# How dense matmuls are shared out over the attention units, and the order of the last output products

## The chip, the cores and the metric

The kernel runs on one NeuronCore of one Trainium2 chip. The metric is the device time of one execution in microseconds (us). TensorE is called PE in the profile, VectorE DVE, ScalarE ACT, GpSimd POOL, and SyncE SP, which issues most of the transfers (DMAs).

## What is computed

The input x (2048 tokens x 1024) is layer-normed, and the sum of three things is returned: x itself, an attention with a memory over the normed x, and a token-mixing MLP over the normed x. The attention, which the change is about, cut to what matters:

```python
# H = 32 heads of Dh = 32, N = 4 segments of L = 512 tokens; q, k, v from x @ wq, wk, wv
for s in range(N):
    logits = einsum('bhqd,bhkd->bhqk', qs, ks) * scale + mask      # causal inside the segment
    a_dot = einsum('bhqk,bhkd->bhqd', softmax(logits), vs)
    a_mem = einsum('bhld,bhde->bhle', phi(qs), M) / (einsum('bhld,bhd->bhl', phi(qs), z) + 1e-6)
    outs.append(g * a_mem + (1 - g) * a_dot)
    M = M + einsum('bhld,bhle->bhde', phi(ks), vs)
    z = z + einsum('bhld->bhd', phi(ks))
out = x + concat(outs) @ wo + mlp                                   # phi(t) = t+1 if t>0 else exp(t)
```

## The kernel before

The MLP and parts of K come first, for about 374 us; their sum with x is left in DRAM as a half-precision partial result (`part_d`). The attention follows, and the change concerns its second part.

**Units.** Attention runs over 32 units u = 0 to 31. Unit u is segment u // 8 and a group of four heads, u % 8. In unit u the kernel computes the *logits* of unit u and the *weighing* (probabilities times values) of unit u - 1. `logits(u, step)` writes PSUM banks 0 to 3: step 0 is key block 0, step 1 is key blocks 1 and 3, and step 2, only in even units, is key block 2 of units u and u + 1 together. After each, one ACT instruction takes exp from the four banks into `pT` (line 1363), and POOL masks the diagonal blocks of `pT` (line 1367). So each logits step has to wait until the exp of the step before has read the banks.

`weigh(u - 1, part)` for parts 0, 1, 2 writes bank 4, 5, 4. After each part DVE copies the bank to `ost` (line 1414). Part 2 therefore waits until the copy of part 0 has been made. In segments 0 to 2 part 2 also updates the memory (`MZ`, lines 1422 and 1424 on DVE).

**Dense jobs.** Between these small products lie jobs of eight dense 128x128x512 matmuls, in banks 6 and 7 by turns (`self.turn`): `v_job` (values, one for each unit up to 27), `q_job` and `k_job` (projections for unit u + 2; from unit 14 on k is loaded from DRAM by `k_load`), and `wo_job`, which is half of an output row block: eight matmuls of `oT` with `wo`, an addition to `fin` on DVE (line 1306), and, for each second half, a transfer of `fin` to the output and a reload of another `fin` with `load_fin`, both issued by SP. There are 24 output jobs for the first three segments. Job n + 2 uses the bank of job n, so it waits for the instruction that empties it: DVE for `k_job` and `wo_job` (and for some early `v_job`), ACT for `q_job` and `v_job`.

**Order.** Everything is written out by hand in program order. `unit_jobs(u)` says which jobs join the queue in unit u. Units 10 to 17 get one output job, put first. From unit 18 on a quota applies: 24 matmuls in even units and 20 in odd ones, filled up with output jobs, put last; what a job has over the quota stays for the next unit (`self.left`). The last unit takes all that is left. `cut` shares the unit's dense matmuls among the places between the small products. In even units the order of places is: before logits 0, before weighing part 0, before part 1, before part 2, before logits 1, before logits 2, before the next unit. Odd units have no logits 2, so there the sixth number is what lies between logits 1 and the end of the unit.

**Side work.** Each unit also leaves a list of VectorE work in `self.side`: scales, products (`prod`, line 1460) and sum (`o_s`, line 1466) of unit u - 1, then `phi_q` and `phi_k` (lines 1227 and 1229), and in some units `xn_scale` (`xs`, line 1133). One item is issued at each stop of a dense job (`STOPS`, or `STOPS_FEW` from unit 14 on, in matmuls of the job), in the places where side work is allowed. DVE runs all of it in the order of issue, with the bank copies and the additions.

**Tail.** After unit 31 the last segment's output is computed in eight products n = 0 to 7 of `product(n, j0, j1)`, each over eight head groups. Seven groups exist early. The last must wait for the weighing of unit 31, its combination on DVE, a transpose on PE (`o_transpose`) and an ACT copy. When a product is complete, DVE adds it to `fin` (line 1617) and the result goes out.

Of the kernel before, what the change touches and what calls it, by code (L numbers as in the profile page):

```python
# [16 lines left out]
N_SEG = 4  # L17
# [13 lines left out]
N_UNIT = N_SEG * N_GRP  # L31
# [355 lines left out]
class _Kernel:  # L387
# [1098 lines left out]
        fw.op("act", lambda e: e.activation(self.oT[s % 3][:, g, :], bb, ACT.Copy),  # L1486
              reads=[self.R_bank[b]], writes=[self.R_oT[s % 3][g]])

    QUOTA_FROM, QUOTA = 18, (24, 20)
    STOPS = ((1, 4, 7), (1, 4))  # L1490
    STOPS_FEW = ((1, 3, 5, 7), (1, 3, 5))
    XN_AT = (0, 1, 2, 3, 6, 7, 8, 9, 14, 15, 16, 17)

    def unit_jobs(self, u):
        jobs = [self.wo_job(*self.wo_jobs.popleft())] if 10 <= u < self.QUOTA_FROM else []
        m = u // 4 + 1
        if m < 2 * N_SEG:
            jobs.append(self.v_job(m, u % 4))
        if u + 2 < N_UNIT:
            jobs.append(self.q_job(u + 2))  # L1500
            if u + 2 < N_UNIT // 2:
                jobs.append(self.k_job(u + 2))
            else:
                self.k_load(u + 2)
        if u >= self.QUOTA_FROM:
            quota = self.QUOTA[u % 2] if u + 1 < N_UNIT else 100
            quota -= 8 * len(jobs) + sum(8 - j[0] for j in self.jobs)
            while quota > 0 and self.wo_jobs:
                jobs.append(self.wo_job(*self.wo_jobs.popleft()))
                quota -= 8  # L1510
            self.left = max(-quota, 0)
        return jobs

    def k_load(self, u):
# [3 lines left out]
    def attention(self):  # L1518
        self.jobs, self.turn, self.left = deque(), 0, 0
        self.side, self.stops = deque(), self.STOPS  # L1520
        self.exps, self.in_etmp = [], [None] * 4
        self.wo_jobs = deque((c, half) for c in range(4 * (N_SEG - 1)) for half in range(2))
        self.jobs.extend([self.q_job(0), self.k_job(0)] + [self.v_job(0, c) for c in range(4)])
        self.dense(16)
        self.late_exps()
        self.phi_k(0)
        self.k_transpose(0)
        self.jobs.extend([self.q_job(1), self.k_job(1)])
        self.dense(100)
        for u in range(N_UNIT):  # L1530
            if u == N_GRP:
                t, R = _Walk(self.mem, self.B_AT + self.STG_AT, self.B_AT + self.S2_AT).take(
                    "oT2", [P, N_GRP, SEG_L], BF16, N_GRP)
                self.oT.append(t)
                self.R_oT.append(R)
                self.load_fin(0)
                self.load_fin(1)
            if 1 <= u <= N_GRP:
                self.fw.dma(self.wo[:, u - 1, :], self.A_wo[(u - 1) * P:u * P, :], writes=[self.R_wo[u - 1]])
            even = u % 2 == 0  # L1540
            self.jobs.extend(self.unit_jobs(u))
            total = 8 * len(self.jobs) - sum(j[0] for j in self.jobs) - self.left
            xn = self.XN_AT.index(u) + 4 if u in self.XN_AT else None
            if u in self.XN_AT[::4]:
                self.xn_load(xn)
                self.xn_load(xn + 1)
            if u < 10 or u >= 14 and total <= 26:
                cuts = self.cut(total, (0, 4, 2, 4, 1, 13, 8) if even else (7, 3, 2, 4, 1, 15))
            else:
                cuts = self.cut(total, (0, 4, 2, 2, 2, 14, 8) if even else (7, 3, 2, 2, 2, 16))  # L1550
            end = u >= N_UNIT - 4
            self.stops = self.STOPS_FEW if total <= 26 and u >= 14 else self.STOPS
            self.dense(cuts[0])
            self.logits(u, 0)
            self.dense(cuts[1], end)
            while end and self.side:
                self.side.popleft()()
            if u:
                self.weigh(u - 1, 0)
            self.dense(cuts[2], False)  # L1560
            if u:
                self.weigh(u - 1, 1)
            self.dense(cuts[3], False)
            if u:
                self.weigh(u - 1, 2)
                steps = self.combine(u - 1)
                last = steps[-1]
                steps[-1] = lambda u=u, last=last: (last(), self.o_transpose_dma(u - 1))
                self.side.append(steps.pop(0))
            if N_GRP <= u:  # L1570
                self.side.append(lambda u=u: self.phi_q(u))
            if u:
                self.side.extend(steps)
            if u + 1 < N_UNIT:
                self.side.append(lambda u=u: (self.phi_k(u + 1), self.k_transpose(u + 1)))
            if xn is not None:
                self.side.append(lambda c=xn: (self.xn_scale(c), self.xn_transpose(c), c % 4 < 2 and self.xn_load(c + 2)))
            self.dense(cuts[4])
            self.logits(u, 1)
            if even:  # L1580
                self.dense(cuts[5])
                self.logits(u, 2)
            self.dense(8 * len(self.jobs) - sum(j[0] for j in self.jobs) - self.left)
        while self.side:
            self.side.popleft()()
        self.tail()
# [10 lines left out]
    def tail(self):  # L1597
        fw = self.fw
        s, u = N_SEG - 1, N_UNIT - 1
        fin, R_fin = self.fin, self.R_fin  # L1600
        for i in range(2, 4):
            self.load_fin(4 * s + i)
        fw.wait_outputs(3)

        def product(n, j0, j1, cols=((0, 512),)):
            i, h, b = n // 2, n % 2, (0, 1, 2, 3, 6, 7, 5, 4)[n]
            for p, (c0, c1) in enumerate(cols):
                with fw.group(reads=self.R_wo[j0:j1] + self.R_oT[s % 3][j0:j1], writes=[self.R_bank[b]]):
                    for jc in range(j0, j1):
                        fw.mm(self.ps[:, b, c0:c1], self.oT[s % 3][:, jc, i * P:(i + 1) * P],  # L1610
                              self.wo[:, jc, h * 512 + c0:h * 512 + c1], start=(jc == 0), stop=(jc == N_GRP - 1))
                if j1 < N_GRP:
                    return
                dst = fin[i][:, h * 512 + c0:h * 512 + c1]
                R = Res("fin")
                R.w = R_fin[i][h].w
                fw.op("dve", lambda e: e.tensor_tensor(dst, self.ps[:, b, c0:c1], dst.bitcast(F16), op=ALU.add),  # L1617
                      reads=[self.R_bank[b], R], writes=[R])
                fw.dma(self.out_d[:, 4 * s + i, h * 512 + c0:h * 512 + c1], dst, reads=[R],
                       is_output=True, issuer=("sp", "act")[p % 2])  # L1620
                b = (b + 1) % 3

        product(0, 0, 6)
        product(1, 0, 6)
        self.weigh(u, 0)
        self.weigh(u, 1)
        product(2, 0, 6)
        self.weigh(u, 2)
        for step in self.combine(u):
            step()  # L1630
        product(3, 0, 6)
        for n in range(3):
            product(n, 6, 7)
        product(4, 0, 7)
        self.o_transpose(u, 4)
        product(3, 6, 7)
        product(5, 0, 7)
        for n in range(6):
            product(n, 7, 8)
        product(6, 0, 8)  # L1640
        product(7, 0, 8, ((0, 256), (256, 384), (384, 512)))

# [27 lines left out]
```

## Time and profile before

| what | value |
|---|---|
| time, median of three runs | 654.52 us (654.16, 654.52 and 1095.52) |
| the profiled execution | 654.28 us |
| its span in the profile | 652.2 us, 11204 instructions |
| matmuls of 128x512, mean as the profile models it | 380 ns |
| exp, line 1363 | 80 times, mean 1877 ns |
| mask on POOL, line 1367 | 128 times, mean 847 ns |
| `prod` on DVE, line 1460 | 24 times, 1215 to 1680 ns |
| addition to `fin` on DVE, line 1306 | 24 times, mean 682 ns |
| granted TensorE clock | 1.0 |

The attention's units begin at 387.48 us in the span, and the tail at about 633.9 us. Matmuls overlap in the pipeline, so the difference of two starts tells more than the durations. In a timeline each row gives the start, the length, the engine, the line, what is written and read, and the number of merged instructions.

### The profile page before, as it was taken

The page shows a single profiled execution, that of the slowest core. Times are in us where ns is not written, and L with a number is a line of the kernel's source. Part 1 is how long each engine was busy: PE and PEld are TensorE (multiplying, and loading weights), DVE is VectorE, ACT ScalarE, POOL GpSimd, SP SyncE. Part 2 cuts the span into 40 slices and gives each one's busy share as a digit, 9 for nine tenths or more (in the row PEclk, how much of TensorE's full clock was granted, in tenths as well). Part 3 has the DMA queues.
Part 4 walks back from the last instruction along what each step waited for, and adds up shares of the span by engine and source line. Part 5 has one row for each costly group of instructions (what it writes and reads, how often), then busy time and mean ns, then how long its engine had stood idle before and what let it go on. Part 6 is the DMA issues. An engine that isn't in the chain of part 4 may idle for free.

```text
span 652.2 us, 11204 instructions
## 1 busy us (share of the span) xinstructions
PE 646.7 (99%) x4611; PEld 303.1 (46%) x4611; DVE 439.9 (67%) x829; ACT 281.5 (43%) x305; POOL 154.9 (24%) x181
## 2 busy tenths in 40 slices
PE   9999999999999999999999999999999999999998
PEld 3444444444444444444444444444545444454444
DVE  6975775665655673745637325767898988887895
ACT  7542232232210000111101047778767788888760
POOL 2500000000011220120201203434333445544450
PEclk9999999999999999999999999999999999999999
DMA  8804242242498937629263956979644576355424
GB/s 300 217 0 130 65 116 79 65 124 70 129 265 216 231 96 210 171 87 258 66 193 116 257 136 156 190 182 227 124 120 109 152 164 144 90 115 123 114 81 138
DMA packets 190123, 95.00 MB, mean 146 GB/s; under 512 B 108664, under 2 KB 176248, under 8 KB 190072
## 3 DMA queue, kind: packets, MB, share of 16 engines
q1 hardware_dynamic: 189928, 94.25, 56.9%
q8 instruction: 36, 0.59, 0.4%
q14 instruction: 15, 0.12, 0.1%
q10 hardware_dynamic: 144, 0.03, 0.0%
HBM read 69.23 MB, written 11.53 MB: 124 GB/s over the span
## 4 chain that ended last, share of the span: by engine, by line
PE 90%; DVE 4%; DMA 2%; ACT 1%; POOL 1%; issue 1%; DVEq 0%
PE ps_all L199 90%; ACT pT L1363 1%; DMA w2s<-in_B_w_dram 1%; POOL pT L1367 1%; DVE fin L1617 1%; DVE ln_st L590 1%; DVE sum L651 0%; DVE prod L1460 0%; DMA xin<-in_A_x_dram 0%; DVE h L630 0%; POOL ln_rs L614 0%; DVE mtmp L1229 0%; DVE mtmp L1227 0%; DVE ost L1414 0%; DVE part L692 0%
## 5 line engine op out<-in xcount | busy, mean ns | idle before, releaser
L1363 ACT ACTIVATE pT<-ps_all 128x2048 bf16<-128x2048 f32 x80 | 150.2, 1877 | 47.2 <-PE ps_all L199 46.8
L1367 POOL TENSOR_SCALAR_AFFINE_SELECT pT<-pT 128x512 bf16<-128x512 bf16 x128 | 106.3, 847 | 160.9 <-ACT pT L1363 160.9
L692 DVE TENSOR_TENSOR part<-ps_all,part 128x512 f32<-128x512 f32 x84 | 57.7, 690 | 108.9 <-PE ps_all L199 88.2
L1078 POOL TENSOR_TENSOR part<-part,stg 128x512 f32<-128x512 f32 x24 | 33.0, 1402 | 285.0 <-DVE part L692 268.1
L749 ACT ACTIVATE g<-part,b1c 128x512 f16<-128x512 f32 x36 | 26.0, 722 | 99.0 <-DVE part L692 99.0
L199 PE MATMUL ps_all<-wv,xnT 128*128 128x512 bf16 x256 | 68.2, 380 | 0.2
L199 PE MATMUL ps_all<-xnT,wq 128*128 128x512 bf16 x256 | 65.6, 380 | 0.0
L199 PE MATMUL ps_all<-wo,oT 128*128 128x512 bf16 (+2 forms) x272 | 64.3, 367 | 0.2 <-ACT pT L1363 0.2
L1414 DVE CAST ost<-ps_all 128x396 bf16<-128x396 f32 (+2 forms) x96 | 44.3, 473 | 27.3 <-PE ps_all L199 26.6
L697 ACT ACTIVATE part<-ps_all 128x512 f32<-128x512 f32 x24 | 14.0, 596 | 101.4 <-PE ps_all L199 67.1
L199 PEld LDWEIGHTS ps_all<-vA,pT 128*128 128x128 bf16 x1280 | 45.5, 96 | 21.5 <-DVE ost L1414 3.3
L199 PE MATMUL ps_all<-g,sum 128*128 128x512 f16 x224 | 51.0, 379 | 0.0
L199 PE MATMUL ps_all<-g,w2s 128*128 128x512 f16 x224 | 51.0, 379 | 0.0
L199 PE MATMUL ps_all<-gT,sum 128*128 128x512 f16 x224 | 50.3, 379 | 0.1
L199 PE MATMUL ps_all<-vA,pT 128*128 128x33 bf16 x1280 | 48.5, 178 | 0.7 <-POOL pT L1367 0.6
L199 PE MATMUL ps_all<-h,sum 128*128 128x512 f16 x192 | 45.2, 379 | 0.0
L199 PE MATMUL ps_all<-h,w1s 128*128 128x512 f16 x192 | 44.9, 379 | 0.0
L199 PE MATMUL ps_all<-hT,sum 128*128 128x512 f16 x192 | 43.6, 379 | 0.0
L199 PEld LDWEIGHTS ps_all<-wo,oT 128*128 128x128 bf16 x272 | 23.8, 97 | 27.1 <-issue 4.9
L1460 DVE TENSOR_TENSOR prod<-ost,srec 128x1024 bf16<-128x1024 bf16 x24 | 35.1, 1461 | 0.0
L199 PEld LDWEIGHTS ps_all<-gT,sum 128*128 128x128 f16 x224 | 21.8, 98 | 26.8 <-DVE gT L666 0.6
L199 PEld LDWEIGHTS ps_all<-g,w2s 128*128 128x128 bf16 x224 | 21.9, 98 | 26.4
(118 smaller groups left out, 862.2 us busy)
## 6 DMA issues: line engine op xcount, KB each, us to landing
w2s<-in_B_w_dram SPq DMA_DIRECT2D x8, 1792.0 KB, 9.5
w1s<-in_B_w_dram SPq DMA_DIRECT2D x12, 1024.0 KB, 5.6
wq<-in_A_wq_dram SPq DMA_DIRECT2D x32, 256.0 KB, 3.4
xs<-in_A_x_dram SPq DMA_DIRECT2D x24, 256.0 KB, 3.4
stg<-in_A_x_dram SPq DMA_DIRECT2D x16, 256.0 KB, 2.8
out_dram<-stg SPq DMA_DIRECT2D x16, 256.0 KB, 3.8
wk<-in_A_wk_dram SPq DMA_DIRECT2D x16, 256.0 KB, 3.4
fin<-out_dram SPq DMA_DIRECT2D x16, 256.0 KB, 3.3
```

Of the source, the lines that this page charges most:

```text
L199: ins = self.nc.tensor.matmul(*args, **kwargs)
L590: fw.op("dve", lambda e: e.bn_stats(st[:, 6 * h:6 * h + 6], src[:, 512 * h:512 * h + 512]), reads=[self.R_xin[c]], writes=[R])
L692: self.fw.op("dve", lambda e: e.tensor_tensor(self.tmp[dst][:], self.bank(b), self.tmp[src][:], op=ALU.add), reads=[self.R_bank[b], self.R ...
L697: self.fw.op("act", lambda e: e.activation(self.tmp[dst][:], self.bank(b), ACT.Copy), reads=[self.R_bank[b]], writes=[self.R_tmp[dst]])
L749: self.fw.op("act", lambda e: e.activation(self.gB[f % 2][half][:, f // 2, :], src, ACT.Gelu_apprx_tanh, bias=self.b1c[:, f:f + 1], scale= ...
L1078: fw.op("pool", lambda e: e.tensor_tensor(self.tmp[t][:], self.tmp[t][:], self.stg[k][:, 512 * half:512 * half + 512], op=ALU.add), reads= ...
L1363: fw.op("act", lambda e: e.activation(dst, src, ACT.Exp, scale=SCALE), reads=self.R_bank[0:4], writes=[R[v % 2][kb] for v, kb, _ in blocks ...
L1367: fw.op("pool", lambda e: e.affine_select(d, d, pattern=[[0, 4], [1, P]], compare_op=ALU.is_ge, fill=0.0, base=0, channel_multiplier=-1), ...
L1414: fw.op("dve", lambda e: e.tensor_copy(dst, src), reads=[self.R_bank[b]], writes=[self.R_ost[o][part]])
L1460: fw.op("dve", lambda e: e.tensor_tensor(self.prod[:], ost[:, :, 0:D_HEAD], rec.unsqueeze(2).to_broadcast([P, 32, D_HEAD]), op=ALU.mult), ...
L1617: fw.op("dve", lambda e: e.tensor_tensor(dst, self.ps[:, b, c0:c1], dst.bitcast(F16), op=ALU.add), reads=[self.R_bank[b], R], writes=[R])
```

## The change

Four things change. Output jobs from unit 10 on all go by quotas, given in rows of four by u % 4: 28 in units 10 to 13, then 24, 24, 24, 20 in units 14 to 21 (20 where u % 4 is 3), then 24 in every unit from 22 to 30. Output jobs are put behind the others, except that in units 28 and 29 the first two jobs change places. From unit 14 on, even units give one matmul more to the place before weighing part 0, and one less to the place before logits 2. In the tail the first product goes to the dense bank that is next in turn instead of bank 0, the others move up accordingly, and product 5 is split after its fifth group, so that the last groups of products 0 to 4 are computed before the rest of it.

```diff
-    QUOTA_FROM, QUOTA = 18, (24, 20)
+    WO_FROM, QUOTA = 10, ((28, 28, 28, 28), (24, 24, 24, 20), (24, 24, 24, 24))
...
     def unit_jobs(self, u):
-        jobs = [self.wo_job(*self.wo_jobs.popleft())] if 10 <= u < self.QUOTA_FROM else []
-        m = u // 4 + 1
+        jobs, m = [], u // 4 + 1
...
-        if u >= self.QUOTA_FROM:
-            quota = self.QUOTA[u % 2] if u + 1 < N_UNIT else 100
+        if u >= self.WO_FROM:
+            quota = self.QUOTA[(u >= 14) + (u >= 22)][u % 4] if u + 1 < N_UNIT else 100
             quota -= 8 * len(jobs) + sum(8 - j[0] for j in self.jobs)
             while quota > 0 and self.wo_jobs:
                 jobs.append(self.wo_job(*self.wo_jobs.popleft()))
                 quota -= 8
             self.left = max(-quota, 0)
+            if m >= 2 * N_SEG and u + 2 < N_UNIT:
+                jobs[0:2] = jobs[1::-1]
...
-            if u < 10 or u >= 14 and total <= 26:
+            if u >= 14 and total <= 26:
+                cuts = self.cut(total, (0, 5, 2, 4, 1, 12, 8) if even else (7, 3, 2, 4, 1, 15))
+            elif u < 10:
                 cuts = self.cut(total, (0, 4, 2, 4, 1, 13, 8) if even else (7, 3, 2, 4, 1, 15))
...
-            i, h, b = n // 2, n % 2, (0, 1, 2, 3, 6, 7, 5, 4)[n]
+            i, h, b = n // 2, n % 2, (6 + self.turn, 0, 1, 2, 3, 7 - self.turn, 5, 4)[n]
...
         product(3, 6, 7)
-        product(5, 0, 7)
-        for n in range(6):
+        product(5, 0, 5)
+        for n in range(5):
             product(n, 7, 8)
+        product(5, 5, 8)
```

## The prediction

> **What bounds the kernel now.** I read the busy shares first, then TensorE's waits, then the chain of waits for the second half, then the timelines of TensorE and VectorE unit by unit.
>
> ```profile
> PE 646.7 (99%) x4611; PEld 303.1 (46%) x4611; DVE 439.9 (67%) x829; ACT 281.5 (43%) x305; POOL 154.9 (24%) x181
> ...
> PE ps_all L199 <- POOL pT L1367: 0.6, 3, 0.3
> PE ps_all L199 <- ACT pT L1363: 0.4, 2, 0.2
> ```
>
> TensorE (PE) is the bound, and the change neither adds nor removes a matmul. Only idle slivers between matmuls can move. The recorded waits are 1.0 us together, but ends of matmuls are modelled, so I measured slivers by starts. Eight dense matmuls back to back take 1.73 us from start to start (0.216 each), a logits block of four to eight takes 0.33, and a step from dense work to logits costs 0.09. What a row takes beyond that is a stall. The chain shows where stalls lie:
>
> ```profile
> 530.92 1.69 DVE prod L1460
> 532.63 0.74 DVE o_s L1466
> 533.37 0.46 DVE xs L1133
> 533.83 0.49 DVE ost L1414
> 534.36 11.84 PE ps_all L199 x133
> ...
> 588.48 1.89 ACT pT L1363
> 590.43 1.35 POOL pT L1367
> 591.92 11.21 PE ps_all L199 x148
> ...
> 631.86 1.89 ACT pT L1363
> 633.89 8.91 PE ps_all L199 x78
> 643.02 2.60 PE ps_all L199 x12
> 646.21 3.60 DVE fin L1617 x7
> ```
>
> Four kinds are to be seen. (1) At 534.36 the last weighing of unit 18 waits for VectorE (DVE) to empty the bank of the first weighing, because VectorE is still on the combination of the unit before. Such waits: 0.18 (unit 15), 0.20 (16), 0.21 (18), 0.09 each (20, 24), together 0.77; and 0.21 in unit 11 for the bank that the kT copy empties. (2) At 588.48 exp runs after an odd unit's second logits; the next logits need its end, and the weighing then needs the mask of POOL. (3) At 631.86 the first tail product needs bank 0, which the last exp still reads. (4) At 646.21 the final additions run back to back on VectorE to the end.
>
> Kind 2 has a measurable rule: from the second logits to the next logits at least 0.45 to the start of exp, 1.88 of exp, 0.14 to the next logits, 2.47 us in all. Nine dense matmuls between give 0.33 + 1.94 + 0.09 = 2.36, so 0.10 is lost; ten give 2.58 and nothing is lost:
>
> ```profile
> 602.70 0.40 PE L199 MATMUL ps_all<-qT,kT 32*128 32x384 bf16 x8
> ...
> 605.17 0.40 PE L199 MATMUL ps_all<-qT,kT 32*128 32x512 bf16 x4
> ...
> 609.00 0.40 PE L199 MATMUL ps_all<-qT,kT 32*128 32x384 bf16 x8
> ...
> 611.60 0.40 PE L199 MATMUL ps_all<-qT,kT 32*128 32x256 bf16 x8
> ```
>
> 605.17 minus 602.70 is 2.47 (nine between), 611.60 minus 609.00 is 2.60 (ten).
>
> **The Trainium skill.** "TensorE: Matmul & The Clock Gate", Back-to-back issue gap, gives N/2.4 + 2.5 ns for a matmul, 216 ns at 512 columns; the trace agrees (0.216). "PSUM — Partial Sum Buffer", Engine vs sequencer instructions: the queues of ScalarE, VectorE and GpSimd are strict FIFO. The chain above agrees: the bank's copy stood 2.9 us behind prod, o_s and xs (530.92 to 533.83). "SBUF — State Buffer", Who interferes with whom: a VectorE instruction with two SBUF inputs and a GpSimd instruction that reads SBUF block each other whole. The trace agrees: prod takes 1.22 us where it starts before the mask and 1.65 to 1.68 where the mask came first.
>
> **The change, part by part.** Worked through by hand, the quotas give the dense matmuls per unit: units 10 to 13, 32 before and 28 after; 15, 24 and 20; 21, 23, 25, 27 and 29, 20 and 24; the others and unit 31 (16) unchanged. That is -16 -4 +20 = 0: 0.216 x 0 = 0.
>
> Longer odd units. Units 21 to 29 get 11 instead of 9 between logits. Five stalls of 0.10 go: -0.50. The later weighing of units 26, 28 and 30 now comes at 0.33 + 2.38 + 0.09 + 0.33 + 0.86 = 3.99 after the logits, and the mask is ready at 591.92 - 588.03 = 3.89. So the mask waits go too, with 0.10 to spare: 0.44, 0.43 and 0.43 (each with the small wait ahead of it), and 0.16 in unit 22, where the dense bank came late from ScalarE: -1.46. Late next is VectorE, below.
>
> One more ahead of the weighing. In even units of 24 the cuts go from 0, 3, 1, 4, 0, 10, 6 to 0, 4, 1, 3, 1, 9, 6. The three ahead of the last weighing still sum to 8, so VectorE's waits there don't feel it, but the ten between second and third logits become nine: by the rule above 0.10 in each of units 14, 16, ... 30, nine times: +0.90. Unit 15, now of 20, pays the same: +0.10.
>
> VectorE in units 11 to 24. The output products come last in a unit instead of first, so their addition (0.60 start to start) lands at other places in VectorE's queue, and 4 fewer or 2 fewer matmuls cover the same queue. Each wait is counted from weighing to weighing. Unit 18: product O5 ends just before its first weighing, so its addition stands ahead of the bank's copy besides xs: 0.21 + 0.60 = 0.81. Unit 16: an addition for xs (+0.14), two matmuls fewer (+0.43), 0.10 of it already paid: 0.67. Unit 15: the same addition, two matmuls fewer: 0.18 + 0.33 = 0.51. Units 12 and 14: two matmuls fewer against a margin of 0.12 and 0.09: 0.31 and 0.34. Units 22 and 24: a new addition (+0.60), two matmuls more (+0.43, of which the stalls just removed take 0.26 and 0.10): 0.60 - 0.17 - 0.12 of slack = 0.31, and 0.09 + 0.60 - 0.33 = 0.36. Unit 20 keeps 0.09. Sum 3.40 for 0.77: +2.63. In unit 11 the kT copy has only the queue of one K job ahead and eight matmuls of cover; I take its 0.21 as gone: -0.21. From unit 26 on, the last weighing has no state update, VectorE idled before the copy, and the added 0.60 costs nothing; if that idle time were gone it would cost up to 0.6 each.
>
> Tail. The first product goes to the bank of the last-but-one output job, whose addition ended at 631.80, long before 633.6: the stall of 0.33 (2.15 for eight matmuls, less 1.73 and 0.09) goes. Its own six matmuls cover exp's end for the second product. The split lets the first final addition start two matmuls (0.43) earlier; the ScalarE copy of the last oT ends at 643.66, and the six matmuls left as cover end at 642.86 + 1.30 = 644.16, so no wait. But the last addition can't start before the last matmul ends at 649.53, against 649.73 now: only 0.17 of the 0.43 counts. -0.50.
>
> Moved with each output job: an output transfer and a reload of fin on SP for each second one. Up to unit 27 they come later than before, from unit 28 at the same place; no PE wait in this stage ends on them, and the first products of the second segment move from unit 18 to 21, away from the oT they need. The swap in units 28 and 29 only exchanges q and an output job. Nothing for either; without that cover a reload (SP issue to landing, 3.3 us) would hold VectorE.
>
> **Sum.** -0.50 - 1.46 + 0.90 + 0.10 + 2.63 - 0.21 - 0.50 = +0.96. The profiled run took 654.28 with a span of 652.2, so 2.1 lie around it, and it stands 0.24 below the median of 654.52. 654.28 + 0.96 = 655.2.
>
> Bounds of what the trace doesn't show: the VectorE waits could stay as they are (-2.63 from the sum, 652.6), since the order of additions may shift by one copy; that they vanish (-0.77 more) I exclude, as no addition leaves the queue of units 15 to 18 without matmuls leaving too, or they could rise by prod taking 1.67 where it takes 1.22 (0.45 in each of units 12 and 14, 0.3 in the three late ones: +1.8, 657.0). The nine stalls of 0.10 could lie inside VectorE's waits in four units (-0.4).
>
> **Rivals.** The waits on VectorE don't grow, since the copy is reached before the addition or the queue is shorter by a prod of 1.22: 652.6. For it speaks that VectorE idles 0.2 to 0.8 ahead of many copies; against it that it didn't in units 15, 16 and 18. The other side: the two engines' block spreads. In units 12, 14 and 26 to 30 the mask comes first, prod goes from 1.22 to 1.67, and the copy follows late: 657.0, clearly slower. It decides where exp ends over 0.45 before prod starts; against it, exp and prod hang on the same weighing and keep their distance. Third, that the extra matmul doesn't do what it says: the longer odd units hide the mask alone, and the part only brings nine stalls. That is in my sum; if the nine don't come, 654.3.
>
> **Numbers.** My account 0.50, its form without the nine stalls 0.12, waits that don't grow 0.23, the spread block 0.12, something unseen 0.03. Range 652.5 to 656.6: the low end takes in the second rival, the upper half of the spread block is left out. A difference of 2% is 13 us, about what a measurement of this kernel tells from none for these chances; the slivers sum to a tenth of that, so faster 0.01, within 0.96, slower 0.03.
>
> **What would show it.** Right: the second to third logits of even units from 14 on 2.47 apart instead of 2.60; no POOL wait ahead of the weighings in units 26, 28, 30; an 0.8 wait ahead of the last weighing in unit 18; no gap ahead of the first tail product; first final addition 0.4 earlier against the tail's transposes, end 0.2. Wrong: VectorE idle ahead of the copies in units 15 to 18, or prod changing its length.

## The result, and the profile after

| what | before | after |
|---|---|---|
| median, six runs of each | 654.46 us | 656.29 us |
| ratio after / before, 95% interval | | 1.0029 [1.0015, 1.0042] |
| span of the profiled execution | 652.2 us | 654.1 us |

One of the six executions of the kernel before took 1095.52 us; the ratio leaves it out. The change costs 1.83 us. The forecast was 655.2 with a range of 652.5 to 656.6; its sum said +0.96. The direction and the range held, but twice the forecast cost was paid, and the parts show why.

The page of the changed kernel gives the busy times, with the number of instructions behind the x.

```profile
span 654.1 us, 11151 instructions
PE 640.5 (98%) x4560; PEld 302.5 (46%) x4611; DVE 440.4 (67%) x829; ACT 281.7 (43%) x305; POOL 153.8 (24%) x181
```

First trap: 4560 matmuls stand beside 4611 weight loads, so 51 records of matmuls are missing here (none were missing before). A missing record lowers the busy time of PE, and a hole just behind a logits block looks like a wait of 0.16. The waits of TensorE in the whole execution (total us, times, longest):

```profile
PE ps_all L199 <- DVE ost L1414: 2.5, 7, 0.6
PE ps_all L199 <- issue: 1.9, 12, 0.2
PE ps_all L199 <- DVE brow L503: 1.3, 1, 1.3
PE ps_all L199 <- DVE fin L1306: 0.8, 2, 0.7
...
PE ps_all L199 <- DVE kT L1261: 0.4, 1, 0.4
PE ps_all L199 <- ACT qT L1252: 0.4, 2, 0.2
```

The twelve waits of the row "issue" are all of this kind. Of the rest, `brow` lies in the MLP and was there before. The two rows on `pT` that the view of before had are gone: the wait for POOL's mask and for the end of exp. In their place stand waits on VectorE: seven for the copy of the first weighing's bank (`ost`), one clear one for an addition of an output job (`fin`, 0.7; the other is beside a hole), one for the K copy (`kT`); and on ScalarE's q copy again one clear one of 0.2 and one of 0.16 beside a hole. Waits under 0.15 are not in this list, in either kernel.

To place the time I took, for each unit, the time from its first logits to those of the next, subtracted the same of before, and took off 0.216 for each dense matmul that the unit had gained (added for each lost). What is left is stall gained or lost (starts are read to 0.01 us, the end of the span to 0.1):

| where | after - before, without the moved matmuls |
|---|---|
| units 10, 13, 17, 19 | 0.00, +0.01, +0.01, +0.01 |
| units 11, 12 | +0.08, +1.19 |
| units 14, 15, 16, 18 | +0.41, +0.74, +0.86, +0.59 |
| units 20, 22, 24 | +0.04, +0.21, +0.25 |
| units 26, 28, 30 | -0.43, -0.42, -0.43 |
| odd units 21 to 29 | -0.12, -0.09, -0.09, -0.09, -0.10 |
| unit 31 and the tail | -0.83 |
| sum | +1.80, against +1.83 measured |

Unit 18 shows the largest wait that had been forecast. VectorE's timeline of the changed kernel (start, length, engine, line, what is written and read):

```profile
529.96 1.68 DVE L1460 TENSOR_TENSOR prod<-ost,srec 128x1024 bf16<-128x1024 bf16 x1
531.68 0.74 DVE L1466 TENSOR_TENSOR o_s<-prod 128x512 bf16<-128x512 bf16 x1
532.34 0.54 DVE L1133 TENSOR_SCALAR xs<-xs,ln_mv,ln_rs 128x1024 bf16<-128x1024 bf16 x1
532.79 0.68 DVE L1306 TENSOR_TENSOR fin<-ps_all,fin 128x512 bf16<-128x512 f32 x1
533.39 1.03 DVE L1414 CAST ost<-ps_all 128x396 bf16<-128x396 f32 x2
```

and TensorE's at the same place:

```profile
532.76 0.59 PE L199 MATMUL ps_all<-wv,xnT 128*128 128x512 bf16 x2
534.00 0.57 PE L199 MATMUL ps_all<-vA,pT 128*128 128x33 bf16 x16 [0.65 <-DVE ost L1414]
```

The `fin` row between `xs` and the copy is new; `prod` keeps its 1.68. The starts 532.79 and 533.39 are 0.60 apart, and unit 18 is 0.59 longer. Unit 15 shows a kind that was not forecast. TensorE there, in the changed kernel:

```profile
509.00 0.22 PE L199 MATMUL ps_all<-MZbf,pqT 128*128 128x132 bf16 x1
509.88 0.59 PE L199 MATMUL ps_all<-xnT,wq 128*128 128x512 bf16 x2 [0.67 <-DVE fin L1306]
```

This is no weighing: a q job waits for its dense bank, because the output job that used the bank before it can't be added yet. The addition comes late through the same queue, behind `prod`, `o_s`, `mtmp` and `xs`. The mask has a small part in it: `mtmp` at 506.89 takes 0.76 here, where it took 0.28 before, as a mask of POOL starts at 506.87 (`xs` after it gets back 0.32, with 0.53 for 0.85). That fits the Trainium skill ("SBUF — State Buffer", Who interferes with whom: an exclusive lock on the port pair that VectorE and GpSimd share, and that `tensor_scalar`, the instruction of `mtmp`, can use in some of its modes).

### The profile page after: what moved, and what is told of

It is laid out like the page before. It is cut to its first block, busy times and chain, and to the rows that moved or that the text cites. A ratio compares the mean times of both kernels' runs of the same rounds, so it can differ in the third digit from the quotient of the medians.

```text
span 654.1 us, 11151 instructions
## 1 busy us (share of the span) xinstructions
PE 640.5 (98%) x4560; PEld 302.5 (46%) x4611; DVE 440.4 (67%) x829; ACT 281.7 (43%) x305; POOL 153.8 (24%) x181
## 4 chain that ended last, share of the span: by engine, by line
PE 88%; DVE 6%; issue 2%; ACT 1%; DMA 1%; SPq 0%
PE ps_all L199 88%; DVE prod L1460 2%; ACT pT L1363 1%; DMA w1early<-in_B_w_dram 1%; DVE ost L1414 1%; DVE mtmp L1227 1%; DVE fin L1306 1%; SPq L221 0%; DVE mtmp L1229 0%; DVE kT L1261 0%; DVE srec L1456 0%; DVE MZbf L1424 0%; DVE o_s L1466 0%; DVE MZ L1422 0%; DVE srec L1457 0%
## 5 line engine op out<-in xcount | busy, mean ns | idle before, releaser
L199 PE MATMUL ps_all<-wv,xnT 128*128 128x512 bf16 x242 | 65.8, 380 | 1.4 <-DVE kT L1261 0.4
L199 PE MATMUL ps_all<-xnT,wq 128*128 128x512 bf16 x238 | 62.4, 380 | 1.2 <-DVE fin L1306 0.7
L199 PE MATMUL ps_all<-wo,oT 128*128 128x512 bf16 (+2 forms) x260 | 60.6, 366 | 1.2 <-issue 0.5
L199 PEld LDWEIGHTS ps_all<-g,sum 128*128 128x128 f16 x224 | 21.9, 98 | 26.4
```

What stands on the lines that cost most here:

```text
L199: ins = self.nc.tensor.matmul(*args, **kwargs)
```

## The experiments

### One part of the change at a time

**The tail alone**: the two hunks in the tail on the kernel before.

```diff
-            i, h, b = n // 2, n % 2, (0, 1, 2, 3, 6, 7, 5, 4)[n]
+            i, h, b = n // 2, n % 2, (6 + self.turn, 0, 1, 2, 3, 7 - self.turn, 5, 4)[n]
...
-        product(5, 0, 7)
-        for n in range(6):
+        product(5, 0, 5)
+        for n in range(5):
             product(n, 7, 8)
+        product(5, 5, 8)
```

> The kernel before with the two edits of the tail alone. By the traces of both kernels the tail is the part that gains: from the last logits to the span's end 0.83 us less than before. Expected 0.8 us faster than before. By the prediction's sum 0.50. A rival, that the tail's gain is only the release of time lost elsewhere in the changed kernel, expects 0 to 0.2.

653.48 against 654.29, -0.81; ratio 0.9989 [0.9982, 0.9995]. The tail's gain stands by itself.

**The cut alone**: only the matmul more ahead of the weighing.

```diff
-            if u < 10 or u >= 14 and total <= 26:
+            if u >= 14 and total <= 26:
+                cuts = self.cut(total, (0, 5, 2, 4, 1, 12, 8) if even else (7, 3, 2, 4, 1, 15))
+            elif u < 10:
```

> The kernel before with only the one matmul more ahead of the first weighing in even units (nine instead of ten ahead of the third logits). The prediction's account: nine stalls of 0.10 (+0.9), less 0.22 in each of the three mask waits of units 26, 28 and 30 (-0.65): 0.25 us slower, second to third logits 2.47 apart. The reading of the changed kernel's trace: no such stalls, second to third logits 2.38 apart, so 0.65 us faster.

655.16, +0.87; ratio 1.0013 [1.0007, 1.002]. Both theories missed. Units 26, 28 and 30 gain 0.21 each, and second and third logits of even units stand 2.38 apart without a stall. But units 20 and 24 lose 0.60 each and unit 15 0.18. Here is VectorE in unit 20 of this kernel:

```profile
547.98 0.74 DVE L1466 TENSOR_TENSOR o_s<-prod 128x512 bf16<-128x512 bf16 x1
548.64 0.68 DVE L1306 TENSOR_TENSOR fin<-ps_all,fin 128x512 bf16<-128x512 f32 x1
549.24 1.03 DVE L1414 CAST ost<-ps_all 128x396 bf16<-128x396 f32 x2
```

and of the kernel before in the same unit:

```profile
547.90 0.74 DVE L1466 TENSOR_TENSOR o_s<-prod 128x512 bf16<-128x512 bf16 x1
548.56 0.56 DVE L1414 CAST ost<-ps_all 128x396 bf16<-128x396 f32 x1
549.04 0.68 DVE L1306 TENSOR_TENSOR fin<-ps_all,fin 128x512 bf16<-128x512 f32 x1
```

The copy and the addition have changed places. A job of eight was left half done with four matmuls to go. With three ahead of the weighing it ends after the first weighing, and its addition is issued behind the copy; with four it ends ahead of it. The strict order of VectorE's queue ("PSUM — Partial Sum Buffer", Engine vs sequencer instructions) then makes TensorE wait 0.60 longer for one matmul that was moved by one place.

**The quotas alone**: `unit_jobs` as in the change, the rest as before.

```diff
-    QUOTA_FROM, QUOTA = 18, (24, 20)
+    WO_FROM, QUOTA = 10, ((28, 28, 28, 28), (24, 24, 24, 20), (24, 24, 24, 24))
...
```

> The kernel before with the quotas and the place of the output jobs alone (no edit of the cuts, none of the tail). If the loss is VectorE's queue in units 11 to 24, as the trace of the changed kernel has it: 1.8 + 0.8 (tail) + 0.3 (the mask waits of units 26, 28, 30 come back in part, at 0.1 each) = 2.9 us slower than before, with the waits in units 11 to 18 as in the changed kernel. If the nine instead of ten matmuls cost 0.9, as predicted, only 2.0 slower.

655.92, +1.63; ratio 1.0025 [1.0016, 1.0034]. It is less than expected because here, too, four left over meet three: in unit 18 the addition (532.38) follows the copy (531.90). Units 16 and 18 take 9.53 and 9.05, where the whole change has 10.12 and 9.65. Unit 12 takes 11.32, as in the whole (11.31). The three parts sum to -0.81 + 0.87 + 1.63 = +1.69, near the whole's +1.83; but the cut's price lies in units 20 and 24 when alone and in 16 and 18 beside the quotas.

### Is it the addition?

**Without six additions**: the changed kernel, in which the output jobs that end before unit 19 aren't added to `fin` (their part is left out of the output).

```diff
-            self.fw.op("dve", lambda e: e.tensor_tensor(dst, self.bank(b), dst.bitcast(F16), op=ALU.add),
-                       reads=[self.R_bank[b], R], writes=[R])
+            if self.u >= 19:
+                self.fw.op("dve", lambda e: e.tensor_tensor(dst, self.bank(b), dst.bitcast(F16), op=ALU.add),
+                           reads=[self.R_bank[b], R], writes=[R])
...
```

> The changed kernel without the six additions to fin of output jobs that end before unit 19; those rows go out without the product. If VectorE's queue makes the waits: unit 18 from 0.81 to 0.2, unit 16 from 0.68 to 0.1, unit 15 from 0.82 to 0.2, unit 11 from 0.38 to 0; the kT wait of unit 12 stays at 0.57 and the 0.61 there stays, for no addition stands ahead of them. In sum 2.1 us faster than the changed kernel. If the waits come from fewer covering matmuls or from exp alone: within 0.3 of the changed kernel.

654.15 against 654.29; ratio 0.9998 [0.9989, 1.0007], so about 2.0 faster than the whole change. Unit 15 goes from 6.72 to 6.09, unit 16 from 10.12 to 9.53, unit 18 from 9.65 to 9.05; unit 11 gives back only 0.16 of the 0.38 that had been expected. Unit 12 stays (11.32 for 11.31): its cost has another cause.

**The addition behind the copy**: nothing is left out, TensorE's order is untouched. The additions of jobs that end just ahead of the first weighing of units 16, 18, 22 and 24 are issued after the copies of the weighing.

```diff
-            self.fw.op("dve", lambda e: e.tensor_tensor(dst, ...), ...)
+            def add(): ...
+            if self.late_add is None: add()
+            else: self.late_add.append(add)
...
+            while self.late_add:
+                self.late_add.pop(0)()
             self.dense(cuts[3], False)
```

> The changed kernel with nothing moved on TensorE; only the four additions of the output jobs that end just ahead of the first weighing of units 16, 18, 22 and 24 are issued to VectorE after that weighing's and the next one's copies. If the place of the addition in VectorE's queue makes these waits: unit 16 from 0.68 to 0.1, unit 18 from 0.81 to 0.2, units 22 and 24 from 0.35 to 0, in sum 1.9 us faster than the changed kernel. If the queue is simply too long: no more than 0.3 faster.

654.63 against 654.42; ratio 1.0003 [0.9994, 1.0012], so 1.6 of the change's 1.83 are gone. VectorE and TensorE in unit 18 of this kernel, where the copy is line 1419 and the addition 1307:

```profile
531.88 0.53 DVE L1133 TENSOR_SCALAR xs<-xs,ln_mv,ln_rs 128x1024 bf16<-128x1024 bf16 x1
...
532.34 1.03 DVE L1419 CAST ost<-ps_all 128x396 bf16<-128x396 f32 x2
532.95 0.57 PE L199 MATMUL ps_all<-vA,pT 128*128 128x33 bf16 x16
533.29 0.67 DVE L1307 TENSOR_TENSOR fin<-ps_all,fin 128x512 bf16<-128x512 f32 x1
```

The copy follows `xs` at once, and the weighing starts 0.61 after it (the row holds the copies of both banks; the weighing needs the first); in the changed kernel it was 532.79 for the addition, 533.39 for the copy, 534.00 for the weighing. Units 16 and 18 fall to 9.53 and 9.05, the values without any addition. Units 22 and 24 only go from 9.41 to 9.27: there the next q job waits some 0.2 for the bank whose addition was put off, which gives part of it back.

### What makes unit 12 long?

Unit 12 has two stalls. The last weighing waits 0.61 for the copy, and a value job waits 0.57 for the bank of the K job (0.41 in the record). TensorE and then VectorE of the changed kernel:

```profile
481.86 0.38 PE L199 MATMUL ps_all<-wv,xnT 128*128 128x512 bf16 x1
482.69 0.57 PE L199 MATMUL ps_all<-vA,pT 128*128 128x33 bf16 x16 [0.45 <-DVE ost L1414]
...
487.93 1.89 PE L199 MATMUL ps_all<-wo,oT 128*128 128x512 bf16 x8
490.23 0.59 PE L199 MATMUL ps_all<-wv,xnT 128*128 128x512 bf16 x2 [0.41 <-DVE kT L1261]
```

```profile
481.47 0.68 DVE L1261 CAST kT<-ps_all 128x512 bf16<-128x512 f32 x1
482.07 1.03 DVE L1414 CAST ost<-ps_all 128x396 bf16<-128x396 f32 x2
...
488.04 0.72 DVE L1227 TENSOR_SCALAR mtmp<-etmp 128x512 bf16<-128x512 bf16 x1
488.79 0.69 DVE L1229 SCALAR_TENSOR_TENSOR mtmp<-kT,mtmp 128x512 bf16<-128x512 bf16 x1
489.40 0.68 DVE L1261 CAST kT<-ps_all 128x512 bf16<-128x512 f32 x1
```

In the first place the K copy stands right ahead of `ost`, 0.60 from start to start; in the second it is itself behind the side work.

**The K copy on ScalarE** from unit 12's K on, in the changed kernel:

```diff
-            fw.op("dve", lambda e: e.tensor_copy(self.kT[k][:], self.bank(b)),
-                  reads=[self.R_bank[b]], writes=[self.R_kT[k]])
+            if u >= 12:
+                fw.op("act", lambda e: e.activation(self.kT[k][:], self.bank(b), ACT.Copy),
+                      reads=[self.R_bank[b]], writes=[self.R_kT[k]])
+            else: ...
```

> The changed kernel with the bank copies of the four k projections for units 12 to 15 on ScalarE instead of VectorE. If VectorE's queue makes the waits of units 12 and 14: the bank wait of 0.57 in unit 12 goes, the 0.61 ahead of its last weighing and the 0.40 of unit 14 go to 0.1 or less, since 0.60 leaves the queue; against that the copy now stands behind the exp of the third logits on ScalarE, which may hold the bank by 0.3 in units 10 and 12. 0.9 us faster than the changed kernel. If the lack of covering matmuls makes them: no change.

655.43 against 654.42; ratio 1.0016 [1.0009, 1.0023], about 0.8 faster than the change by the medians, and 0.5 by the sum of its units. Units 11, 12 and 14 get shorter by 0.38, 0.40 and 0.40, but unit 10 goes from 10.12 to 10.80. ScalarE and then TensorE there:

```profile
468.91 1.88 ACT L1367 ACTIVATE pT<-ps_all 128x2048 bf16<-128x2048 f32 x1 [0.66 <-PE ps_all L199]
...
471.20 0.59 ACT L1262 ACTIVATE kT<-ps_all 128x512 bf16<-128x512 f32 x1
471.85 0.61 PE L199 MATMUL ps_all<-wv,xnT 128*128 128x512 bf16 x2 [0.51 <-ACT kT L1262]
```

The K copy has left one queue for another: on ScalarE it stands behind an exp of 1.88 and a further 0.62 for `etmp` (left out above), though the K job's last matmuls began at 468.79, and unit 12 keeps a bank wait of 0.76. So the K copy's place ahead of `ost` is shown as a cause in units 11, 12 and 14; the second stall of unit 12 was only moved.

### How many matmuls does exp need between two logits?

**Eight between**: the changed kernel with two matmuls more ahead of the second logits and two less ahead of the third.

```diff
-                cuts = self.cut(total, (0, 5, 2, 4, 1, 12, 8) if even else (7, 3, 2, 4, 1, 15))
+                cuts = self.cut(total, (0, 5, 2, 4, 3, 10, 8) if even else (7, 3, 2, 4, 1, 15))
```

> The changed kernel with eight instead of nine matmuls between second and third logits of even units from 14 on (two more go ahead of the second logits). Eight give 0.33 + 1.73 + 0.09 = 2.15 of work. If these logits need 2.47 as between odd and even units, 0.32 is lost nine times: 2.9 us slower than the changed kernel, the gap at 2.47. If the need is smaller in even units, the gap shows it directly: at 2.38, 2.0 us slower.

657.84 against 654.42; ratio 1.0053 [1.0038, 1.0068], 1.6 more than the change. TensorE in unit 28, first of the changed kernel with its nine (seven and two), then of this one with its eight:

```profile
611.60 0.40 PE L199 MATMUL ps_all<-qT,kT 32*128 32x384 bf16 x8
...
613.99 0.40 PE L199 MATMUL ps_all<-qT,kT 32*128 32x256 bf16 x8
```

```profile
612.90 0.40 PE L199 MATMUL ps_all<-qT,kT 32*128 32x384 bf16 x8
...
615.28 0.40 PE L199 MATMUL ps_all<-qT,kT 32*128 32x256 bf16 x8 [0.15 <-ACT pT L1363]
```

2.39 with nine, which is what the work takes (0.33 + 9 x 0.216 + 0.09 = 2.36) within 0.03; 2.38 with eight, whose work takes 2.15. So exp asks for 2.38 here, and nine just cover it. The nine even units lose 0.21 each; unit 15 gains 0.32 by the side.

### A version without the new waits

**Tail and late cut**: the kernel before with the change's tail, and with its cut only where no state update follows.

```diff
-            if u < 10 or u >= 14 and total <= 26:
+            if u >= 26 and total <= 26:
+                cuts = self.cut(total, (0, 5, 2, 4, 1, 12, 8) if even else (7, 3, 2, 4, 1, 15))
+            elif u < 10 or u >= 14 and total <= 26:
...
```

> The kernel before with the tail's edits and the cut of one more matmul only from unit 26 on, where the mask waits are and the last weighing has room. From the two runs of the parts: -0.81 for the tail, -0.64 for the mask waits, and none of the waits of units 15, 20 and 24: 1.45 us faster than before.

653.01 against 654.42, -1.41; ratio 0.998 [0.9973, 0.9988]. Units 26 and 28 go from 9.02 to 8.80, unit 30 from 9.04 to 8.84.

**Queue order**: the same, and in three places work is issued behind the copies of the weighing: the addition of the output job in unit 15, and `xs` of units 15 and 17 (which ran in 16 and 18).

```diff
...
+            self.hold = u == 15
             self.dense(cuts[1], end)
+            self.hold = False
...
+            while self.late:
+                self.late.pop(0)()
             self.dense(cuts[3], False)
...
-                self.side.append(lambda c=xn: ...
+                (self.late if u in (15, 17) else self.side).append(lambda c=xn: ...
```

> The kernel before with the tail's edits, the cut of one more matmul from unit 26 on, and a changed order on VectorE only in units 15 to 18: the addition of the output job that ends ahead of the first weighing of unit 15, and the scaling xs of units 15 and 17, are issued after the copies of the next first two weighings. If what stands ahead of the copy makes the waits of units 15, 16 and 18 (0.18, 0.20, 0.21), they go: 0.55 us faster than the tail and the late cut alone, 2.0 faster than before. If VectorE is simply full there: no gain over 1.4.

652.35 against 654.37, -2.02; ratio 0.9969 [0.9957, 0.9981]. It is the fastest kernel of the study, with the quotas of before. Its page, and its TensorE waits in full:

```profile
PE 646.0 (99%) x4611; PEld 303.0 (47%) x4611; DVE 440.4 (68%) x829; ACT 281.5 (43%) x305; POOL 154.8 (24%) x181
```

```profile
PE ps_all L199 <- DVE brow L503: 1.3, 1, 1.3
PE ps_all L199 <- ACT pT L1368: 0.2, 1, 0.2
```

No wait on `ost`, `fin` or `kT` is recorded; none was in the kernel before either, where those waits are seen by the starts alone, so the unit times have to tell. Units 15, 16 and 18 fall by 0.19, 0.22 and 0.22, about the stalls that before had there. VectorE's busy time is 440.4, against 440.2 with the tail and the late cut: in these units not the amount of its work but its order made the difference.

## Why the prediction was right, and where it was not

| term of the sum | predicted | measured | |
|---|---|---|---|
| longer odd units 21 to 29 | -0.50 | -0.49 | right |
| masks of units 26, 28, 30, small wait of 22 | -1.46 | about -1.44 | right |
| ten become nine in even units | +0.90 | 0 | failed |
| odd nine in unit 15 | +0.10 | +0.10 | right |
| waits on VectorE, units 11 to 24 | +2.42 | about +4.43 | size wrong |
| tail | -0.50 | -0.83 | more than sized |

The measured column is from the table by units. Two terms meet in units 15 and 22. In unit 15 the second logits and the next stand 2.47 apart with nine matmuls between, so 0.10 is lost there. In unit 22 the first value matmul starts 0.33 after the logits, where before it was 0.49, so the 0.16 went.

**The step that failed outright** is "the ten between second and third logits become nine: by the rule above 0.10 in each". The rule of 2.47 was read from odd units (unit 19 of the changed kernel still shows it: 543.41 to 545.88), and used for even ones, where 2.38 is enough. The counts of nine and ten shown in the prediction could not tell the two apart: ten never stalled. The two cases don't have the same logits after exp (4 instructions of 512 columns against 8 of 256), but what makes up the 0.09 stayed open: exp starts 0.45 after the logits and takes 1.88 in both. No run put eight matmuls at the odd place, and the profile records no wait on exp there, so it is not shown that the 2.47 is exp's need; that two matmuls more remove the 0.10 is shown (odd units 21 to 29).

**The term that was mis-sized** is VectorE. Units 14, 18, 22 and 24 came out as worked (0.41 for 0.34, 0.59 for 0.60, 0.37 for 0.31, 0.25 for 0.27). Unit 20 came out near its sum by luck: it was to keep its wait of 0.09 on the copy, but that went, and a dense bank comes 0.16 late there, as it did in unit 22 before. The rest of the 2.0:

- Unit 12, +0.88 more. "Two matmuls fewer against a margin of 0.12" counts wrong: the cut of 28 gives 14 for 16 ahead of the first logits and 7 for 8 up to the last weighing, so three matmuls, 0.65 - 0.12 = 0.53, near the 0.61 measured. And the "eight matmuls of cover", for which the prediction took the wait of unit 11 as gone, were not counted for unit 12: there the K copy waits behind side work, and eight were too few by 0.57. The K copy's part ahead of `ost` is shown by moving it to ScalarE; the count of three is worked out only.
- Unit 11, +0.29 more: the wait for the K copy's bank went (0.30 by the starts, not the 0.21 that the prediction read), but its last weighing now waits 0.38 for the copy.
- Unit 15, +0.31 more: the addition does not only delay the next copy, it holds the dense bank of the q job after it. Shown by leaving the additions out (6.72 to 6.09).
- Unit 16, +0.39 more: the addition's part came as forecast (0.68 for 0.67, and the unit falls by 0.59 with the copy first). The other 0.38 lies before the next logits: a value job waits for the bank of the q copy, which ScalarE runs after exp (`qT` at 522.94, the job at 523.59). The prediction did not look at that bank's cover; no run isolates it.

The remark that "the three ahead of the last weighing still sum to 8, so VectorE's waits there don't feel it" is wrong as well. It counts matmuls between logits and the last weighing, but not at which of them a job ends. In the whole change this is why units 16 and 18 have the addition ahead of the copy; the prediction had the right order in both and booked it under the quotas.

**The tail** gained 0.33 more than sized. The split did what was forecast: the first final addition starts 1.94 after the transposes instead of 2.37 (0.43), of which 0.16 reach the last addition (0.17 forecast). The stall ahead of the first product went as well, but it was mis-sized. The eight matmuls at 631.74 are followed by the first product at 633.89, so 2.15 for 1.73; the further 0.09 that the prediction took off is a step from dense work to logits, and none stands there. This gave 0.40 for the 0.33. Unforeseen was the rest. From the start of the last addition to the end, where only output transfers run, all eight profiles with the new tail take 2.24 to 2.26 and all three with the old one 2.49; why was not tested. And 0.06 came from a wait for the transfer that brings unit 30's output into `oT`, ahead of the seventh groups (0.16 before, 0.10 after). These four make 0.86 (the 0.83 is by spans that are printed to 0.1). The last wait differs between profiles with the same new tail: it is nothing with eight between, and 0.65 with the K copy on ScalarE (recorded as 0.49):

```profile
642.55 2.33 PE L199 MATMUL ps_all<-wo,oT 128*128 128x512 bf16 x10 [0.49 <-DMA oT<-o_s]
```

The pieces of the tail were not tested one by one.

The errors cancel in part: -0.90 for exp's need, +2.01 for VectorE and -0.33 for the tail make +0.78 of the 0.87 that the sum missed; the rest is rounding of the terms. That the time fell within the range owes something to this luck: without the false +0.90 the same sum would have said +0.06, or 654.3. The rival in which `prod` grows from 1.22 to 1.67 is out: in all the units that it names, 12, 14 and 26 to 30, `prod` keeps 1.22 (and 1.68 in unit 18). The block by POOL did show, but on `mtmp`, in unit 15.

## What to carry to other kernels

Here one engine is saturated, and most of the cost of moving its work was decided in the in-order queues of the engines that empty its buffers. In such a kernel, for each such copy, write out what stands ahead of it before and after the move, and at which matmul each job ends. An addition that nothing waits for belongs behind the copy that the busy engine waits for, as long as its own bank isn't needed first. A least distance measured at one place (2.47) is to be measured again at each other place where it decides (2.38).

## What was not expected of the hardware

Unit times repeat to about 0.02 us from one kernel to another where the order is the same (unit 12: 11.31 to 11.32 in five kernels; unit 18: 9.05 to 9.06 in three), so single stalls of 0.1 can be read from starts even where some matmul records are missing. From one logits block to the next with little work between, 2.38 us pass in even units (eight matmuls) and 2.47 in odd ones (nine). And from unit 10 on `mtmp`, an instruction with one input, took 0.28 or 0.29 in both kernels where no mask of POOL was running or one began within 0.01 of it, and 0.72 to 0.76 where a mask had begun 0.02 or more ahead.
